# An attention softmax whose norms move ahead of the score diagonals, and value loads and transposes moved a period later

**The chip and the metric.** The kernel runs on one core of a Trainium2 chip. The time is the device time of one execution in microseconds (us), and where one number stands for several executions it is the median. A run is called slow when it is more than 1.5% above the fastest run of its kernel; medians and ranges below keep such runs, ratios leave them out. Engines are named as the profile names them: PE multiplies matrices, PEld loads its weights, DVE, ACT and POOL work on vectors, SP issues transfers. "PEq" and "SPq" are the instruction queues of PE and SP.

## The reference

Four batches of 6208 rows and 256 columns go through two stages. The attention is over channels, so its score matrix is 256 x 256 per batch, and its norms run over all rows.

```python
qn = q / (np.linalg.norm(q, axis=1, keepdims=True) + 1e-06)
kn = k / (np.linalg.norm(k, axis=1, keepdims=True) + 1e-06)
s = kn.transpose(0, 2, 1) @ qn / tau          # 256 x 256 per batch
a = softmax(s)                                # cut: written out in the reference
x = v @ a
x_prev = x moved down by one row              # cut
xk = mu_k * x + (1.0 - mu_k) * x_prev
xr = mu_r * x + (1.0 - mu_r) * x_prev
k = np.maximum(xk @ w_k, 0.0)                 # 256 -> 1024
out = sigmoid(xr @ w_r) * (k * k @ w_v)       # 1024 -> 256
```

## The kernel before

Nothing of `x` can be computed before the scores of its batch are complete, so the kernel has two parts. In the first some 34 us it reads all of q and k of batch 0, and sums the covariance and the squares as the rows land. Then comes a serial stretch: norms, square roots, scaling, transposes of the scaled scores, exp, weights, first product. After that 48 blocks of 512 rows follow one another, twelve per batch and a remainder. A stretch of work for one block is called a period here, some 10 us. The covariance of batches 1 to 3 is woven into the periods of the batch before.

The covariance of batch 0 in its last group of rows, and the norms, which came after everything else. The square of a query norm is a diagonal entry of q times q, and the diagonals are taken by a multiplication with the identity and a sum:

```python
def cov_first(g, diagonal=None):
    ...
    if last:
        for s in range(n):
            for ih in range(2):
                c = slice(at[ih], at[ih] + P)
                nc.tensor.matmul(cov[0][ih][:, c], row[:, s, c], row[:, s, c], ...)
        diagonal()
    ...
def norms_first():          # 22 matmuls of one column: sums of squares of k
    bank[0] = ps.tile([P, 4], F32, name="bank", tag="xT_ps", bufs=2)
    ...
def diagonals():
    for h in range(2):
        nc.vector.tensor_tensor(dg[:, h], cov[0][h][:, ...], ident_f, op=OP.mult)
    nc.vector.tensor_reduce(rn[:, 0:2], dg, axis=AX, op=OP.add)
```

The serial stretch, in program order:

```python
norms_first()
... # loads of v, w_k, w_r, w_v and of the next groups are issued
root(0)                                              # of the queries
root(1)                                              # of the keys
nc.scalar.activation(gate, ones[:, 0:1], AF.Exp)     # brings the exp table in
invert_first(0)
evac_first()                                         # scaling of the scores
go = v_transpose_pe(0, nc.vector.tensor_copy)        # v of block 0, on PE
...
turn()                                               # transposes of the scores
invert_first(1)
go()
...
exp()
v_transpose_pe(1, nc.scalar.copy)()
keep_warm(2)                                         # filler matmuls
weigh_first(0)
weigh_first(1)
...
```

In the main loop the v of a block is loaded by POOL (in bf16), transposed from one on-chip buffer into another by a transfer that SP issues, and used in the product `xT`. The results of a block go out by a store that SP issues too.

```python
if j == 0 and 4 <= i + 6 < NBLK - 1:
    v_load(i + 6)                  # v_bf: 6 buffers
...
if j == 5 and 4 <= i + 5 < NBLK - 1:
    v_transpose(i + 5)             # vT: 5 buffers, issued on SP
...
stores.append((dst, res))          # res: 6 slots; the first stores are held back (HOLD = 4)
while len(stores) > max(0, HOLD - max(0, i - 3)):
    nc.sync.dma_start(*stores.pop(0))          # issued on SP
```

Of the kernel before, what the change touches and what calls it, by code (L numbers as in the profile page):

```python
# [18 lines left out]
def kernel(  # L19
# [115 lines left out]
    def group_cast(g, between):  # L135
# [6 lines left out]
        else:  # L142
# [3 lines left out]
                              f[0][:rows, :n].rearrange("p s (x c) -> p s x c", c=P))  # L146
        if between:
            between.pop(0)()
# [29 lines left out]
    def cov_first(g, diagonal=None):  # L178
# [7 lines left out]
# [4 lines that stand above are left out]
                    nc.tensor.matmul(cov[0][ih][:, c], row[:, s, c], row[:, s, c], start=False, stop=s == n - 1,  # L190
                                     skip_group_check=True)
            diagonal()
        for s in range(n):
            for ih in range(2):
                c = slice(P, 3 * P) if last else slice(ih * P, ih * P + 3 * P)
                nc.tensor.matmul(cov[0][ih][:, c], row[:rows, s, at[ih]:at[ih] + P], row[:rows, s, c],  # L196
                                 start=g == 1 and s == 0, stop=last and s == n - 1, skip_group_check=True)

    def norms_first():

        bank[0] = ps.tile([P, 4], F32, name="bank", tag="xT_ps", bufs=2)
# [3 lines left out]
        for g in [0] + list(range(DIRECT, LAST + 1)):  # L205
            rows, n = rows_of(0, g)
            k2 = groups[0, g][1] if g else rowsum["left"]
            for s in range(n):
                for h in range(2):
                    nc.tensor.matmul(bank[0][:, h:h + 1], k2[:rows, s, h * P:(h + 1) * P], ones[:rows, 0:1],  # L210
                                     start=False, stop=g == LAST and s == n - 1, skip_group_check=True)
# [68 lines left out]
    def softmax_pieces(b):  # L280
# [18 lines left out]
        def diagonals():  # L299
            dg = pn.tile([P, 2, P], F32, name="dg", tag="dg", bufs=1)  # L300
            for h in range(2):
                nc.vector.tensor_tensor(dg[:, h], cov[0][h][:, 3 * P * h:3 * P * h + P], ident_f, op=OP.mult)
            nc.vector.tensor_reduce(rn[:, 0:2], dg, axis=AX, op=OP.add)
# [64 lines left out]
    L1 = L + 1  # L368
    HOLD = 4
# [6 lines left out]

    def v_load(i):
        b, t = blocks[i]
        v_bf = p2.tile([P, S, C], BF16, name="v_bf", tag="v_bf", bufs=6)
# [4 lines left out]
    def v_transpose(i):  # L384

        v_bf = st.pop((i, "v"))
        vT = p2.tile([P, S, 2, P], BF16, name="vT", tag="vT", bufs=5)
# [3 lines left out]
    def v_transpose_pe(i, evac):  # L391
# [7 lines left out]
        if i == 0:  # L399
            return lambda: evac(vT0[:, :, 1:].rearrange("c h (s p) -> c s h p", s=S), vT_ps)  # L400
        vT = p2.tile([P, S, 2, P], BF16, name="vT", tag="vT", bufs=5)
        st[i, "vT"] = vT
        if i == 3:
# [4 lines left out]
                            vT_ps.rearrange("c s h p -> c h p s"))  # L408

# [17 lines left out]

    H = M // 2
# [202 lines left out]
    for g in order(0):  # L631
        if (0, g) not in groups:
            group_load(0, g)
        if g == LAST:
            nc.sync.dma_start(mu_rows[0:2], moe_mu_k.rearrange("(h p) -> h p", p=P))
            nc.sync.dma_start(mu_rows[2:4], moe_mu_r.rearrange("(h p) -> h p", p=P))
        group_cast(g, pending)
        pending = k_sum(g) if 0 < g < DIRECT else []
        cov_first(g, diagonals)
        if g == NB - 1:  # L640

            nc.gpsimd.tensor_copy(gate, groups[0, g][0][:, 0, 0:1])
            v_load(0)
    norms_first()
# [52 lines left out]
    difference, product = x_first()  # L697
    root(0)
    root(1)
    nc.scalar.activation(gate, ones[:, 0:1], AF.Exp)  # L700
    invert_first(0)
    evac_first()
    go = v_transpose_pe(0, nc.vector.tensor_copy)
    mu_ps = ps.tile([P, 4], F32, name="mu_ps", tag="kT_ps", bufs=3)
    nc.tensor.transpose(mu_ps, mu_rows, ident_f[:4, :4])
    turn()
    invert_first(1)
    go()
    nc.vector.tensor_copy(mu_t, mu_ps)
# [3 lines left out]
    v_transpose_pe(1, nc.scalar.copy)()  # L713
    keep_warm(2)
# [15 lines left out]
    for i in range(-2, NBLK - 1):  # L730
        for j in range(8):
# [5 lines left out]
            if j == 0 and 4 <= i + 6 < NBLK - 1:  # L737
                v_load(i + 6)
# [41 lines left out]
            if j == 5 and 4 <= i + 5 < NBLK - 1:  # L780
                v_transpose(i + 5)
# [63 lines left out]
```

## Time and profile before

| | before |
|---|---|
| time, median of 3 runs | 505.6 us (505.32 to 506.75) |
| span of the profiled execution | 504.6 us, mean granted clock 0.997 |
| PE busy | 480.1 us, 95% |
| DVE and ACT busy | 85% each |
| PE wait from 60 to 490 us | none listed |
| last k of batch 0 landed | 34.47 us |

The lines themselves are shown and read in the prediction. The granted clock of PE is 1.00 when full and 0.50 when halved. A mean clock of 0.997 over 504 us means that one window of 3.41 us at half clock fell into this execution (half of 3.41 us is 1.7 us, and 1.7/504 is 0.0034). The trace places it from 38.29 to 41.70 us.

### The profile page before, as it was taken

The numbers are of one execution on the slowest core, as the hardware profiler recorded it, in microseconds if no ns is written. First come the engines' busy times: TensorE is split into PE (matmuls) and PEld (weight loads), VectorE is DVE, ScalarE is ACT, GpSimd is POOL, SyncE is SP. The second block draws the span as 40 slices with busy tenths as digits, with TensorE's granted clock in tenths as the row PEclk, the third lists the DMA queues.
The fourth block names the chain that finished last, engine by engine and source line by source line (L and its number), as shares of the span: only waits on it lengthen the run. The fifth ranks groups of instructions, "written<-read, shape, count | busy, mean of one in ns | idle before, by whom it ended". The sixth has DMA issues, their size and how long they took to land.

```text
span 504.6 us, 9229 instructions
## 1 busy us (share of the span) xinstructions
PE 480.1 (95%) x3370; PEld 332.0 (66%) x3429; DVE 430.1 (85%) x788; ACT 428.4 (85%) x869; POOL 96.7 (19%) x143
## 2 busy tenths in 40 slices
PE   1689999999999999999999999999999999999996
PEld 0355667667676676767676676667666666666675
DVE  2787899999989999899889899899988787878784
ACT  3778999899989988888999898988888878888784
POOL 0044332222233223112133322100031000000000
PEclk9998999999999999999999999999999999999999
DMA  8999999999999999997699999972296854452123
GB/s 323 419 314 198 196 164 163 159 201 205 232 216 161 215 172 170 163 185 115 141 188 156 177 189 185 162 155 63 64 205 113 153 98 110 81 100 70 54 73 105
DMA packets 131542, 83.46 MB, mean 165 GB/s; under 512 B 50532, under 2 KB 125608, under 8 KB 130472
## 3 DMA queue, kind: packets, MB, share of 16 engines
q0 software_dynamic: 55824, 33.01, 51.0%
q1 hardware_dynamic: 75352, 49.59, 42.8%
q8 instruction: 27, 0.44, 0.4%
q10 hardware_dynamic: 320, 0.26, 0.2%
q14 instruction: 19, 0.16, 0.1%
HBM read 78.71 MB, written 25.43 MB: 206 GB/s over the span
## 4 chain that ended last, share of the span: by engine, by line
PE 82%; DVE 6%; ACT 5%; DMA 5%; issue 2%; SPq 0%; POOL 0%; DVEq 0%; ACTq 0%
PE vr_ps L564 31%; PE kT_ps L532 28%; PE vr_ps L560 9%; PE xT_ps L424 7%; PE s_ps L277 5%; DMA f<-in_k_dram 4%; DVE kk L545 1%; ACT kr L537 1%; DVE xk L517 1%; ACT k L158 1%; DMA v_bf<-in_v_dram 1%; ACT sq L235 1%; DVE res L574 1%; ACT qk L153 1%; DVE delta L507 0%
## 5 line engine op out<-in xcount | busy, mean ns | idle before, releaser
L537 ACT ACTIVATE kr<-kT_ps 128x512 bf16<-128x512 f32 (+1 forms) x390 | 234.5, 603 | 33.6 <-PE kT_ps L532 29.7
L564 PE MATMUL vr_ps<-w_v_sb,kk 128*128 128x256 bf16 x1536 | 230.2, 273 | 0.4
L532 PE MATMUL kT_ps<-xk,w_k_sb 128*128 128x512 bf16 (+1 forms) x722 | 217.6, 377 | 0.3 <-DVE xk L517 0.2
L564 PEld LDWEIGHTS <-kk 128*128 128x128 bf16 x1536 | 150.3, 98 | 57.3
L545 DVE TENSOR_TENSOR kk<-kr 128x2048 bf16<-128x2048 bf16 (+1 forms) x148 | 125.8, 851 | 0.2 <-ACT kr L537 0.2
L574 DVE SCALAR_TENSOR_TENSOR res<-res,vr_ps 128x256 f32<-128x256 f32 x192 | 80.0, 417 | 50.2 <-ACT res L573 50.2
L532 PEld LDWEIGHTS <-w_k_sb 128*128 128x128 bf16 x780 | 75.5, 98 | 27.5 <-issue 0.6
L573 ACT ACTIVATE res<-vr_ps 128x256 f32<-128x256 f32 x192 | 76.4, 398 | 1.3 <-PE vr_ps L564 1.3
L560 PE MATMUL vr_ps<-w_r_sb,xr 128*128 128x256 bf16 x384 | 73.3, 273 | 2.5
L426 ACT CAST xT<-xT_ps 128x512 bf16<-128x512 f32 x94 | 55.9, 594 | 20.0 <-PE xT_ps L424 19.6
L517 DVE SCALAR_TENSOR_TENSOR xk<-delta,mu_t,xT 128x512 bf16<-128x512 bf16 x94 | 70.0, 746 | 0.0
L517 DVE SCALAR_TENSOR_TENSOR xr<-delta,mu_t,xT 128x512 bf16<-128x512 bf16 x94 | 70.0, 746 | 0.0
L560 PEld LDWEIGHTS <-xr 128*128 128x128 bf16 x384 | 37.6, 98 | 44.6 <-issue 0.2
L133 POOL DMA_DIRECT2D qk<-in_q_dram x39 | 26.0, 667 | 161.8 <-ACT kr L537 142.9
L424 PE MATMUL xT_ps<-vT,a_sb 128*128 128x512 bf16 x188 | 55.9, 379 | 0.0
L277 PE MATMUL s_ps<-qk 128*128 128x256 bf16 (+1 forms) x294 | 55.8, 273 | 0.0
L238 ACT ACTIVATE sq<-qk 128x1024 bf16<-128x1024 bf16 x48 | 51.0, 1062 | 0.0
L380 POOL DMA_DIRECT2D v_bf<-in_v_dram x48 | 36.5, 764 | 50.5 <-DMA vT<-v_bf 39.7
L196 PE MATMUL s_ps<-qk 128*128 128x384 bf16 (+2 forms) x98 | 19.7, 349 | 16.3 <-ACT qk L153 15.4
L507 DVE TENSOR_TENSOR delta<-xT 128x1024 bf16<-128x1024 bf16 x47 | 32.3, 686 | 1.1 <-ACT xT L426 1.1
L277 PEld LDWEIGHTS <-qk 128*128 128x128 bf16 (+1 forms) x294 | 28.5, 98 | 5.6 <-issue 0.8
L133 POOL DMA_DIRECT2D qk<-in_k_dram x39 | 25.8, 662 | 8.2 <-DMA v_bf<-in_v_dram 3.5
(110 smaller groups left out, 252.7 us busy)
## 6 DMA issues: line engine op xcount, KB each, us to landing
out_dram<-res SPq DMA_DIRECT2D x47, 512.0 KB, 4.8
v_bf<-in_v_dram POOLq DMA_DIRECT2D x48, 256.0 KB, 8.4
qk<-in_q_dram POOLq DMA_DIRECT2D x36, 256.0 KB, 7.2
qk<-in_k_dram POOLq DMA_DIRECT2D x36, 256.0 KB, 8.8
f<-in_q_dram SPq DMA_DIRECT2D x4, 1024.0 KB, 13.5
f<-in_k_dram SPq DMA_DIRECT2D x4, 1024.0 KB, 11.0
f<-in_q_dram SPq DMA_DIRECT2D x3, 512.0 KB, 7.7
f<-in_k_dram SPq DMA_DIRECT2D x3, 512.0 KB, 6.2
```

What stands on the lines that cost most here:

```text
L133: nc.gpsimd.dma_start(rows_at(qk, b, g, i)[:rows, :n], qk_src(t, b, g))
L277: nc.tensor.matmul(s_ps[:, ih, :], rows_at(qk, b, g, 0)[:rows, s, ih * P:(ih + 1) * P], rows_at(qk, b, g, 1)[:rows, s, :], start=t0 and ih ...
L424: nc.tensor.matmul(xT_ps, a_sb[:, b, ih, dh * P:(dh + 1) * P], vT[:, :, ih, :], start=ih == 0, stop=ih == 1)
L426: nc.scalar.copy(xT[:, dh, 1:], xT_ps)
L517: nc.vector.scalar_tensor_tensor(o[:, dh], st[i, "d"][:, dh], mu[:, dh:dh + 1], st[i, "x"][:, dh, :M], op0=OP.mult, op1=OP.add)
L532: nc.tensor.matmul(kT_ps[:, :m], w_k_sb[:, dh, fh * P:(fh + 1) * P], xk[:, dh, :m], start=dh == 0, stop=dh == 1)
L537: nc.scalar.activation(kr, kT_ps[:, :m], AF.Relu, scale=0.5 ** 0.5)
L545: nc.vector.tensor_tensor(st[i, "kk"][:, fh // 4 * 4 + lo:fh + 1, :m], kr, kr, op=OP.mult)
L560: nc.tensor.matmul(vr_ps[:, D:], xr[:, dh, s * P:(s + 1) * P], w_r_sb[:, dh, :], start=dh == 0, stop=dh == 1)
L564: nc.tensor.matmul(vr_ps[:, :D], kk[:, fh, s * P:(s + 1) * P], w_v_sb[:, fh, :], start=fh == 0, stop=fh == 7)
L573: nc.scalar.activation(res[:, s], vr_ps[:, D:], AF.Tanh, scale=0.5)
L574: nc.vector.scalar_tensor_tensor(res[:, s], res[:, s], 1.0, vr_ps[:, :D], op0=OP.add, op1=OP.mult)
```

## The change

The intent has two parts. In the start, everything that the exp table waits for is moved forward, and the v of block 0 comes in two halves. In the main loop v is loaded and transposed one period later, so that two transposed buffers do and fewer transfers queue up. Its core, with cuts:

```diff
 def cov_first(g, diagonal=None):
             diagonal()
+            norms_last()            # 4 of the 22 norm matmuls, behind the diagonals
...
-            nc.vector.tensor_tensor(dg[:, h], cov[0][h][:, ...], ident_f, op=OP.mult)
-        nc.vector.tensor_reduce(rn[:, 0:2], dg, axis=AX, op=OP.add)
+            nc.vector.scalar_tensor_tensor(dg[:, h], cov[0][h][:, ...], 1.0, ident_f,
+                                           op0=OP.mult, op1=OP.mult, accum_out=rn[:, h:h + 1])
...
+        if g == LAST:
+            norms_first()           # the other 18, ahead of the last group
         group_cast(g, pending)
         cov_first(g, diagonals)
         if g == NB - 1:
-            nc.gpsimd.tensor_copy(gate, groups[0, g][0][:, 0, 0:1])   # POOL marker
             v_load(0)               # after: a DVE memset marks it; loaded in two halves
-norms_first()
...
-    root(0)
     root(1)
+    root(0)
     nc.scalar.activation(gate, ones[:, 0:1], AF.Exp)
+    nc.tensor.transpose(bank[0][:, 4:8], mu_rows, ident_f[:4, :4])
+    keep_warm(2)
+    turn_half, take_half = v_first()
     invert_first(0)
     evac_first()
-    go = v_transpose_pe(0, nc.vector.tensor_copy)
...
+    turn_half(0)
     turn()
+    turn_half(1)
+    go = v_transpose_pe(1, nc.scalar.copy)
+    keep_warm(3)
     invert_first(1)
-    go()
+    take_half(0, nc.vector.tensor_copy)
...
     exp()
-    v_transpose_pe(1, nc.scalar.copy)()
-    keep_warm(2)
+    take_half(1, nc.scalar.copy)
+    go()
...
-            if j == 0 and 4 <= i + 6 < NBLK - 1:
-                v_load(i + 6)                       # v_bf: 6 buffers
+            if j == 0 and 4 <= i + 5 < NBLK - 1:
+                v_load(i + 5)                       # 5 buffers
...
-            if j == 5 and 4 <= i + 5 < NBLK - 1:
-                v_transpose(i + 5)                  # vT: 5 buffers
+            if j == 5 and 4 <= i + 4 < NBLK - 1:
+                v_transpose(i + 4)                  # 2 buffers
```

The line numbers shift. L190 (diagonal matmuls) becomes L192, L203 and L210 (norms) L206 and L217, L306 (roots) L317, L316 (scaling) L327, L337 (transposes of the scores) L348, L345 (exp) L356, L448 (first product) L482, L388 (transposes by transfer) L411, L573 and L581 (tanh into the result, store) L607 and L615.

More of the change, by code (lines that the diff above doesn't have):

```diff
@@ L146, in group_cast @@
                               f[0][:rows, :n].rearrange("p s (x c) -> p s x c", c=P))
+        if g == NB - 1:
+            v_mark()
         if between:
@@ L199, in norms_first @@
     def norms_first():
-        bank[0] = ps.tile([P, 4], F32, name="bank", tag="xT_ps", bufs=2)
+        bank[0] = ps.tile([P, 8], F32, name="bank", tag="xT_ps", bufs=2)
         for h in range(2):
@@ L204, in norms_first, with norms_of, norms_last @@
                              start=h == 0, stop=False, skip_group_check=True)
-        for g in [0] + list(range(DIRECT, LAST + 1)):
-            rows, n = rows_of(0, g)
-            k2 = groups[0, g][1] if g else rowsum["left"]
-            for s in range(n):
-                for h in range(2):
-                    nc.tensor.matmul(bank[0][:, h:h + 1], k2[:rows, s, h * P:(h + 1) * P], ones[:rows, 0:1],
-                                     start=False, stop=g == LAST and s == n - 1, skip_group_check=True)
+        for g in [0] + list(range(DIRECT, LAST)):
+            norms_of(g)
+    def norms_of(g):
+        rows, n = rows_of(0, g)
+        k2 = groups[0, g][1] if g else rowsum["left"]
+        for s in range(n):
+            for h in range(2):
+                nc.tensor.matmul(bank[0][:, h:h + 1], k2[:rows, s, h * P:(h + 1) * P], ones[:rows, 0:1],
+                                 start=False, stop=g == LAST and s == n - 1, skip_group_check=True)
+    def norms_last():
+        norms_of(LAST)
     def half_tile(name, shape, dtype, tag):
@@ L301, in diagonals @@
             for h in range(2):
-                nc.vector.tensor_tensor(dg[:, h], cov[0][h][:, 3 * P * h:3 * P * h + P], ident_f, op=OP.mult)
-            nc.vector.tensor_reduce(rn[:, 0:2], dg, axis=AX, op=OP.add)
+                nc.vector.scalar_tensor_tensor(dg[:, h], cov[0][h][:, 3 * P * h:3 * P * h + P], 1.0, ident_f,
+                                               op0=OP.mult, op1=OP.mult, accum_out=rn[:, h:h + 1])
         def root(h):
@@ L368 @@
     L1 = L + 1
+    H = M // 2
     HOLD = 4
@@ L375, in size, with v_mark @@
         return M if i < NBLK - 1 else B * L
+    def v_mark():
+        st["mark"] = p2.tile([P, S, C], BF16, name="v_bf", tag="v_bf", bufs=5)
+        nc.vector.memset(st["mark"][0:1, 0, 0:1], 0.0)
     def v_load(i):
         b, t = blocks[i]
-        v_bf = p2.tile([P, S, C], BF16, name="v_bf", tag="v_bf", bufs=6)
+        v_bf = st.pop("mark") if i == 0 else p2.tile([P, S, C], BF16, name="v_bf", tag="v_bf", bufs=5)
+        if i == 0:
+            for a in range(2):
+                nc.gpsimd.dma_start(v_bf[:, 2 * a:2 * a + 2], v[b, a * H:(a + 1) * H, :].rearrange(
+                    "(s p) c -> p s c", p=P))
+            st[i, "v"] = v_bf
+            return
         nc.gpsimd.dma_start(v_bf, v[b, t * M:(t + 1) * M, :].rearrange(
@@ L386, in v_transpose @@
         v_bf = st.pop((i, "v"))
-        vT = p2.tile([P, S, 2, P], BF16, name="vT", tag="vT", bufs=5)
+        vT = p2.tile([P, S, 2, P], BF16, name="vT", tag="vT", bufs=2)
         nc.sync.dma_start_transpose(vT.rearrange("c s h p -> c (s h) p"), v_bf.rearrange("p s c -> p (s c)"))
@@ L397, in v_transpose_pe @@
                 nc.tensor.transpose(vT_ps[:, s, h], v_bf[:, s, h * P:(h + 1) * P], ident)
-        if i == 0:
-            return lambda: evac(vT0[:, :, 1:].rearrange("c h (s p) -> c s h p", s=S), vT_ps)
-        vT = p2.tile([P, S, 2, P], BF16, name="vT", tag="vT", bufs=5)
+        vT = p2.tile([P, S, 2, P], BF16, name="vT", tag="vT", bufs=2)
         st[i, "vT"] = vT
@@ L408, in v_transpose_pe, with v_first, turn_half, take_half @@
                             vT_ps.rearrange("c s h p -> c h p s"))
+    def v_first():
+        v_bf = st.pop((0, "v"))
+        vT_ps = ps.tile([P, S, 2, P], BF16, name="vT_ps", tag="kT_ps", bufs=3)
+        def turn_half(a):
+            for s in (2 * a, 2 * a + 1):
+                for h in range(2):
+                    nc.tensor.transpose(vT_ps[:, s, h], v_bf[:, s, h * P:(h + 1) * P], ident)
+        def take_half(a, copy):
+            copy(vT0[:, :, a * H + 1:(a + 1) * H + 1].rearrange("c h (s p) -> c s h p", s=2),
+                 vT_ps[:, 2 * a:2 * a + 2])
+        return turn_half, take_half
     def x_half(i, dh):
@@ L426, in x_half @@
         nc.scalar.copy(xT[:, dh, 1:], xT_ps)
-    H = M // 2
     def x_first():
@@ L697 @@
     difference, product = x_first()
+    root(1)
     root(0)
-    root(1)
     nc.scalar.activation(gate, ones[:, 0:1], AF.Exp)
+    nc.tensor.transpose(bank[0][:, 4:8], mu_rows, ident_f[:4, :4])
+    keep_warm(2)
+    turn_half, take_half = v_first()
     invert_first(0)
     evac_first()
-    go = v_transpose_pe(0, nc.vector.tensor_copy)
-    mu_ps = ps.tile([P, 4], F32, name="mu_ps", tag="kT_ps", bufs=3)
-    nc.tensor.transpose(mu_ps, mu_rows, ident_f[:4, :4])
+    turn_half(0)
     turn()
+    turn_half(1)
+    go = v_transpose_pe(1, nc.scalar.copy)
+    keep_warm(3)
     invert_first(1)
-    go()
-    nc.vector.tensor_copy(mu_t, mu_ps)
+    take_half(0, nc.vector.tensor_copy)
+    nc.vector.tensor_copy(mu_t, bank[0][:, 4:8])
     nc.vector.tensor_scalar_add(less, mu_t, -1.0)
```

## The prediction

> **What bounds the kernel now.** I first read the busy totals, then the list of waits, then the windows, and then the timeline of the start. The page's totals and its costliest matmul groups:
>
> ```profile
> PE 480.1 (95%) x3370; PEld 332.0 (66%) x3429; DVE 430.1 (85%) x788; ACT 428.4 (85%) x869; POOL 96.7 (19%) x143
> ...
> L564 PE MATMUL vr_ps<-w_v_sb,kk 128*128 128x256 bf16 x1536 | 230.2, 273 | 0.4
> L532 PE MATMUL kT_ps<-xk,w_k_sb 128*128 128x512 bf16 (+1 forms) x722 | 217.6, 377 | 0.3 <-DVE xk L517 0.2
> ```
>
> PE is busy 95% of the span, and its two large groups waited 0.7 us in all (the numbers after the second bar). The list of PE's waits confirms it: its longest entry is 15.4 us for the ACT cast of L153, and its window from 60 to 490 us lists no PE wait at all. So after the start the kernel runs at the pace of the matmul stream. Two whole periods (one period is one block of 512 rows) from the windows view; the columns are window, length, busy time of PE, PEld, DVE, ACT and POOL, then granted clock, DMA share and GB/s:
>
> ```profile
> 110.44:120.55 10.11, 10.01 (x76) 7.18 (x76) 9.78 (x19) 9.28 (x20) 3.79 (x6) 1.00 1.34 203
> 343.06:352.74 9.68, 9.58 (x72) 6.79 (x72) 8.76 (x17) 8.56 (x19) 0.00 (x0) 1.00 0.38 82
> ```
>
> The first has 20 matmuls of 512 columns and 52 of 256 (six covariance units in it), the second 8 fewer of 256. Both are full; the DMA engines are saturated in the first (share above 1) and idle most of the time in the second.
>
> What is left to win is the start, the first 50 us, where one chain goes through several engines. The end of it, from the timeline (start, duration, engine, line):
>
> ```profile
> 34.88 0.39 PE L190 MATMUL s_ps<-qk 128*128 128x128 bf16 x4
> 35.24 0.49 DVE L302 TENSOR_TENSOR dg<-s_ps,ident_f 128x128 f32<-128x128 f32 x2 [0.32 <-PE s_ps L190]
> 35.77 0.42 DVE L303 TENSOR_REDUCE rn<-dg 128x2 f32<-128x256 f32 x1
> 36.11 0.50 PE L203 MATMUL bank<-ones_f,k_acc 128*128 128x1 f32 x4
> 36.93 0.88 DVE L316 TENSOR_SCALAR s_sb<-s_ps,rn 128x256 f32<-128x256 f32 x2
> 37.27 0.17 ACT L306 ACTIVATE rn<-bank 128x2 f32<-128x2 f32 x1 [0.84 <-PE bank L210]
> 37.41 0.62 PE L397 MATMUL vT_ps<-ident,v_bf 128*128 128x128 bf16 x8 [0.18 <-DMA v_bf<-in_v_dram]
> 37.46 1.28 ACT L700 ACT_TABLE_LOAD   x1
> 38.11 0.99 PE L337 MATMUL st_ps<-ident_f,s_sb 128*128 128x128 f32 x4
> 39.14 0.47 ACT L345 ACTIVATE e_sb<-st_ps,rn 128x256 f32<-128x256 f32 x1 [0.18 <-PE st_ps L337]
> 40.60 0.64 PE L448 MATMUL x_ps<-vT,a_sb 128*128 128x256 bf16 x2 [0.22 <-DVE sm L357]
> ```
>
> The key norms and roots come after everything else, the v of block 0 holds PE until 37.4, and the transposes of the scaled covariance (L337) release exp. From 38 to 42 us PE runs at half clock, which the windows view shows:
>
> ```profile
> 34.70:38.10 3.40, 2.90 (x42) 2.33 (x39) 2.60 (x11) 1.52 (x4) 3.40 (x6) 1.00 1.16 171
> 38.10:41.60 3.50, 3.28 (x19) 2.59 (x20) 2.50 (x10) 2.77 (x7) 1.15 (x2) 0.53 1.08 190
> ```
>
> **What the Trainium skill says.** "TensorE: Matmul & The Clock Gate", Back-to-back issue gap, gives N/2.4 + 2.5 ns for a warm matmul. An estimate for the first period above is then 20 x 0.2158 + 52 x 0.1092 = 9.99 us; the trace has 10.0 to 10.1, so it agrees, and the stream holds no slack to win. The same page, Part 1: The HAM clock gate, says the clock is halved after a window of about 3.4 us with little PE activity, and that the window runs freely. The trace agrees: 0.53 for 3.5 us, and matmuls of 128 columns 0.107 us apart in it against 0.056 before. "ScalarE: Activation LUTs", What ACT_TABLE_LOAD costs, gives 1283 ns for the load; the trace has 1.28. "DMA: Bandwidth & Descriptors", Queues, rings and completion order, says each DMA engine takes turns between queue rows and consumes one ring in order. The trace agrees in so far as transposes issued behind stores landed late: 17.5 us after issue for the one at 110.9 us, against 3.1 at the least in a quiet stretch.
>
> **The change, part by part.**
>
> Norms ahead. The instruction order shows 18 tiny matmuls (4 f32 passes, then 14 of k squares) moved in front of L190. Before, the 22 tiny matmuls took from 36.11 to 37.1, so the 18 take about 0.9 us. PE is continuously busy up to L190 (its L196 matmuls run from 32.88 into 34.88), so nothing hides them: L190 goes from 34.88 to about 35.75, a loss of 0.9 on the path to the diagonals.
>
> Diagonals. The multiply with accumulated sum removes the reduce: 35.24 to 36.19 is 0.95 us now, about 0.55 after. A gain of 0.4. The query root would then come at about 36.7 instead of 36.2.
>
> Roots. With the key root first (at about 36.4) and the query root last (until 36.9), the table load starts at about 36.95, not 37.46, a gain of 0.5 on ACT: ready for exp at 38.45, not 38.96.
>
> v of block 0. Its marker is one DVE memset after an early cast, in place of a POOL copy that waited for the key cast and ended at 32.28; the first half may be issued at about 31.9, not 32.4, and lands by my estimate at 35.5. So L337 no longer stands behind eight transposes. It waits for the scaled covariance: invert and scaling start 0.45 later than now (36.93 to about 37.4), its two halves are ready at 37.9 and 38.3, and the transposes end at about 38.7 with a full clock, 38.95 with half. They end at 39.1 now. Exp thus gains 0.15 to 0.4 us.
>
> After exp. Two bf16 copies stand on ACT (half of v, 0.55 us, and the v of block 1, 1.01 us) before the first xT cast, which can start near 41.4 at best against 42.00 now. Three filler matmuls stand before the first product. With a full clock they and the 12 transposes cost 0.65 + 0.67 us and end at about 40.0, before the weights are ready. With half clock they cost 1.28 + 1.28, and the first product starts at 41.4, not 40.6. So the sum of the start is a gain of about 0.6 us if the clock stays up, and a loss of about 0.6 if not. The two fillers added at about 37 raise activity by 0.43 us in a window of 3.4; I cannot tell from one trace whether this is enough, and call it 60 to 40 for it. Expected: 0.6 x 0.6 - 0.4 x 0.6 = 0.1 us gained, and with the relief of the first DMA burst (one v load and one transpose fewer before 60 us) I call it 0.3.
>
> Later v. No instruction more or less. The two vT buffers tie a transpose for block n to the end of the product of block n-2. Its lead is two periods less the 3.2 us that this product is spread over: 16.8 us where the period is 10, 16 later. In the trace landing takes 4 to 11 us after 140 us, so 5 us or more remain. Between 60 and 130 us landing took 16.4 to 19.1 us from issue. That is not service time alone: three transposes stood in one ring, and they landed 6 to 10 us apart. Issued one per period they should land in 7 to 10 us up to 100 us, and in 13 to 16 behind two stores of 512 KB each around 110 to 140 us. Slack is thus 1 to 8 us: tight, but positive, so I count nothing for it.
>
> **Sum**: 505.6 - 0.3 = 505.3; I say 505.2.
>
> **Rivals.**
> 1. Late vT. If a transpose lands in 18 us as now, PE waits about 1 us in each of the periods from 60 to 140 us, and up to 10 us in all: 507 to 515. For it: the landing times. Against it: with fewer transposes queued the ring is shorter, and total DMA work by any moment falls.
> 2. Half clock with fillers in the way: 506.2, as worked out above. For it: 0.53 in the window. Against it: the fillers were put there to prevent it.
> 3. The start gains more: no half clock at all, and the later v frees the burst for weights and q, k: 504.0. For it: DMA share above 1 from 42 to 130 us. Against it: from 60 us on no PE wait is listed, so earlier data has nothing to shorten there.
>
> **Range and chances.** 2% is 10 us. The start can give little more than 1.5 us, as PE is full from 50 us on, so faster by 2% is all but excluded. Only rival 1 in its worst form reaches 2% slower. The range 503.6 to 507.2 holds rivals 2 and 3 and a mild form of rival 1.
>
> **What would show it.** L190's counterpart starts near 35.75; the table load near 36.95; exp near 38.8; the first product near 40.1 (right) or 41.4 (rival 2); the granted clock from 38 to 41.6 near 1 or near 0.5. A list of PE waits from 60 us on with entries for the vT transposes would prove rival 1, and periods between 60 and 140 us above 10.1 us would size it. If block 3's product starts later than 60.3 us with the clock up, my reading of the start is wrong.

## The result

| | before | after |
|---|---|---|
| time in the same rounds | 506.18 us (505.32 to 507.29, 4 runs) | 505.73 us (505.47 to 506.17, 4 runs) |
| ratio, 95% interval | | 0.9991 (0.9967 to 1.0015): same |
| span and clock, profiled | 504.6 us, 0.997 | 503.7 us, 0.998 |

A ratio is the mean time of one kernel's fast runs over that of the other's of the same rounds, so it is not quite the ratio of the medians. The output is correct. The medians differ by less than the runs of one kernel do. What differs more is the scatter, and the experiments return to it.

The page of the changed kernel has the busy totals, and the groups, almost unchanged. The columns of the groups are: line, engine, operation, count, then busy time, mean ns of one, and idle time before them.

```profile
PE 479.2 (95%) x3372; PEld 331.1 (66%) x3432; DVE 428.9 (85%) x790; ACT 428.7 (85%) x870; POOL 97.0 (19%) x143
...
L598 PE MATMUL vr_ps<-w_v_sb,kk 128*128 128x256 bf16 x1536 | 230.3, 273 | 0.1
L566 PE MATMUL kT_ps<-xk,w_k_sb 128*128 128x512 bf16 (+1 forms) x721 | 217.3, 377 | 0.4 <-DVE xk L551 0.2
```

The two groups of matmuls stand at 230.3 and 217.3 us, as before. PE lists no wait from 60 to 490 us in this kernel either. The windows of the start do differ: the granted clock (the seventh number after the window) is now full in the second one, where it was 0.53.

```profile
34.70:38.10 3.40, 2.98 (x39) 2.28 (x39) 1.75 (x9) 1.99 (x5) 3.40 (x7) 1.00 1.00 137
38.10:41.60 3.50, 3.01 (x29) 2.14 (x29) 2.39 (x11) 2.78 (x9) 1.27 (x2) 1.00 1.03 164
```

These lines are picked out of the serial stretch in the timeline of the changed kernel (start, duration, engine, line; the bracket is idle time before the instruction and what ended it):

```profile
34.69 0.50 PE L206 MATMUL bank<-ones_f,k_acc 128*128 128x1 f32 x4
35.26 0.45 PE L217 MATMUL bank<-ones,k 128*128 128x1 bf16 x12
35.57 0.38 PE L192 MATMUL s_ps<-qk 128*128 128x128 bf16 x4
35.94 0.29 DVE L313 SCALAR_TENSOR_TENSOR dg<-s_ps,ident_f 128x128 f32<-128x128 f32 x1 [1.27 <-PE s_ps L192]
36.37 0.08 DVE L313 DVE_READ_ACCUMULATOR dg<-s_ps,ident_f 128x1 f32 x1
36.71 1.28 ACT L734 ACT_TABLE_LOAD   x1
37.74 0.83 PE L348 MATMUL st_ps<-ident_f,s_sb 128*128 128x128 f32 x4
38.41 0.39 PE L439 MATMUL vT_ps<-ident,v_bf 128*128 128x128 bf16 x4
38.61 0.47 ACT L356 ACTIVATE e_sb<-st_ps,rn 128x256 f32<-128x256 f32 x1 [0.40 <-PE st_ps L348]
38.83 0.42 DVE L442 COPY vT<-vT_ps 128x512 bf16<-128x512 bf16 x1 [0.48 <-PE vT_ps L439]
39.97 0.35 DVE L369 TENSOR_SCALAR a_sb<-e_sb,sm 128x256 bf16<-128x256 f32 x1
40.38 0.39 PE L482 MATMUL x_ps<-vT,a_sb 128*128 128x256 bf16 x2 [0.49 <-DVE a_sb L369]
```

The norms (L206, L217) run from 34.69 until the diagonal matmuls (L192) can start at 35.57, so they cost 0.88 us with nothing beside them. The table load then starts at 36.71, not 37.46, and exp at 38.61, not 39.14. Yet the first product starts at 40.38, only 0.22 us sooner than before, and the last k alone landed 0.27 us sooner in this run (34.20 against 34.47). Counted from that landing, the first product is 0.05 us **later** than before (6.18 against 6.13 us).

The reason is in the line of L442. DVE's copy of the first half of v starts when the PE transposes of the *second* half end (38.41 + 0.39 = 38.80), although it needs only the first: both halves lie in one tile. That copy and the work queued behind it put the weights (L369) at 39.97, and PE waited 0.49 us for them. The runs norms_mid and better, below, test this: with both halves in one tile the copy starts at 38.32, when the second half's transposes have ended, and with a tile for each it starts at 37.90, before those transposes begin (38.09).

The gain that the profile does show comes after that. The product of block 1 starts 9.60 us after the last k, against 10.07 before, because PE is no longer at half clock from 38.29 to 41.70. The product of block 3 then keeps that distance: 25.32 against 25.79. So the 0.9 us between the two spans are 0.47 from the start, 0.27 from the landing of the data, and 0.16 from the rest.

In the main loop, the instruction queue of SP looks different. First before, then after, picked from the timeline (L388 and L411 are transposes, L581 and L615 are stores; the second number is how long the issue took):

```profile
93.60 4.84 SPq L581 DMA_DIRECT2D out_dram<-res  x2
98.55 9.90 SPq L388 DMA_TRANSPOSE vT<-v_bf  x1
108.54 2.23 SPq L581 DMA_DIRECT2D out_dram<-res  x2
```

```profile
92.94 1.23 SPq L411 DMA_TRANSPOSE vT<-v_bf  x1
94.27 1.49 SPq L615 DMA_DIRECT2D out_dram<-res  x2
102.93 1.33 SPq L411 DMA_TRANSPOSE vT<-v_bf  x1
104.31 1.66 SPq L615 DMA_DIRECT2D out_dram<-res  x2
```

Before, a transpose took 9.90 us merely to be issued, and two stores took 4.84 us. After, it is 1.2 to 1.3 us and 1.5 to 1.7 us. The transposes issued between 90 and 125 us landed 17.5 to 18.3 us after issue before, and 4.5 to 7.5 us after. PE sees none of this in these two profiles; the experiments show where it matters.

### The profile page after: what moved, and what is told of

The parts are those of the page before. It is cut to its first block, busy times and chain, and to the rows that moved or that the text cites. A ratio compares the mean times of both kernels' runs of the same rounds, so it can differ in the third digit from the quotient of the medians.

```text
span 503.7 us, 9236 instructions
## 1 busy us (share of the span) xinstructions
PE 479.2 (95%) x3372; PEld 331.1 (66%) x3432; DVE 428.9 (85%) x790; ACT 428.7 (85%) x870; POOL 97.0 (19%) x143
## 4 chain that ended last, share of the span: by engine, by line
PE 90%; DMA 4%; ACT 2%; DVE 2%; issue 1%; SPq 0%; ACTq 0%; DVEq 0%
PE vr_ps L598 33%; PE kT_ps L566 30%; PE vr_ps L594 10%; PE xT_ps L460 8%; PE s_ps L288 6%; DMA f<-in_k_dram 4%; ACT k L160 1%; ACT qk L155 1%; PE s_ps L199 1%; PE st_ps L348 0%; PE y_ps L638 0%; DVE xk L551 0%; DVE k L167 0%; DVE kk L579 0%; ACT kr L508 0%
## 5 line engine op out<-in xcount | busy, mean ns | idle before, releaser
L598 PE MATMUL vr_ps<-w_v_sb,kk 128*128 128x256 bf16 x1536 | 230.3, 273 | 0.1
L566 PE MATMUL kT_ps<-xk,w_k_sb 128*128 128x512 bf16 (+1 forms) x721 | 217.3, 377 | 0.4 <-DVE xk L551 0.2
L607 ACT ACTIVATE res<-vr_ps 128x256 f32<-128x256 f32 x192 | 76.6, 399 | 1.3 <-PE vr_ps L598 1.3
```

What stands on the lines that cost most here:

```text
L566: nc.tensor.matmul(kT_ps[:, :m], w_k_sb[:, dh, fh * P:(fh + 1) * P], xk[:, dh, :m], start=dh == 0, stop=dh == 1)
L598: nc.tensor.matmul(vr_ps[:, :D], kk[:, fh, s * P:(s + 1) * P], w_v_sb[:, fh, :], start=fh == 0, stop=fh == 7)
L607: nc.scalar.activation(res[:, s], vr_ps[:, D:], AF.Tanh, scale=0.5)
```

## The experiments

Two questions are to be told apart. Theory: the new start saves nothing of its own and only avoids a half-clock window, and the later v is what keeps the scatter away. Rivals: the new order of the start is itself worth about half a microsecond; or the later v is neutral, as the prediction counted it. The expectations for the first runs still favoured these rivals, and v_only and start_only speak against them.

All times of the start below are counted from the landing of the last k in the same profile, because that landing moves by up to 0.5 us from run to run (34.16 to 34.68 us) and has nothing to do with the change. Every kernel gave a correct result.

| kernel | exp | first product | block 1 | block 3 | block 9 | half clock in the start |
|---|---|---|---|---|---|---|
| before | 4.67 | 6.13 | 10.07 | 25.79 | 86.08 | 3.41 us |
| after | 4.41 | 6.18 | 9.60 | 25.32 | 85.62 | none |
| after_again | 4.44 | 6.21 | 9.63 | 25.36 | 85.65 | none |
| start_only | 4.49 | 6.25 | 9.71 | 25.44 | 88.25 | none |
| v_only | 4.20 | 5.45 | 8.87 | 24.59 | 84.89 | none |
| before_warm | 4.53 | 5.73 | 9.16 | 24.88 | 85.70 | none |
| tr_only | 4.55 | 6.31 | 9.74 | 25.46 | 85.75 | none |
| hold2 | 4.43 | 6.20 | 9.62 | 25.35 | 85.64 | none |
| more_res | 4.36 | 6.13 | 9.55 | 25.27 | 85.56 | none |
| norms_mid | 3.86 | 5.65 | 9.46 | 25.18 | 85.47 | none |
| better | 3.79 | 5.55 | 9.39 | 25.11 | 85.40 | none |
| better_one | 4.79 | 6.17 | 9.62 | 25.35 | 85.64 | none |
| after_nofill | 4.31 | 8.10 | 12.84 | 28.56 | 88.85 | 6.83 us |

The columns are the start of the instruction in question in us: exp, the first product of block 0, and the first product of blocks 1, 3 and 9.

### The changed kernel again

No edit; this only sets the scatter, in five rounds.

> The changed kernel unaltered, to size the difference and to see how often each kernel drops to half clock at the start. Theory (the start alone gains, part of it by keeping the clock up): ratio to the kernel before 0.998 to 1.000, first product of block 0 about 40.4 us after the start of the span, block 3's first xT product near 59.5 us (60.26 before), no half clock between 30 and 60 us in any profile. Rival (the 0.9 us between the two spans is chance, of the load phase and of where a free-running clock window happens to fall): ratio 1.000 within 0.1%, and the granted clocks of the two kernels' runs spread alike.

Measured: 505.75 us (505.62 to 506.03, 6 runs). The kernel before, in the same rounds, had a median of 505.79 and a range of 505.04 to 513.03 in 11 runs; the ratio is 0.9975 (0.9926 to 1.0024). The medians are equal, and the lowest run of before is below the lowest of the changed kernel by 0.58 us. Four of the eleven runs of before were 507 us or more. So the change does not make a good run better, and the next runs ask what it does to a bad one.

### The new start with the old v, and the old start with the new v

start_only has the changed kernel's start, and the loads, transposes and buffers of the old loop:

```diff
-name="v_bf", tag="v_bf", bufs=5        # after
+name="v_bf", tag="v_bf", bufs=6
-name="vT", tag="vT", bufs=2
+name="vT", tag="vT", bufs=5
-v_load(i + 5) ... v_transpose(i + 4)
+v_load(i + 6) ... v_transpose(i + 5)
```

v_only is the reverse: the same four edits the other way round, made to the kernel before.

> The changed start with the old v schedule (v loaded and transposed one period earlier, 6 and 5 buffers). Theory (all of the gain is the start): within 0.1% of the changed kernel, block 3's product near 59.5 us, and the transposes of 60 to 130 us land 16 to 19 us after issue again. Rival (the later v gives the gain by relieving the first burst): block 3's product back near 60.2 us, time back to that of the kernel before.

> The old start with the new v schedule (one period later, 5 and 2 buffers). Theory: same time as the kernel before within 0.1%, block 3's product near 60.3 us, no PE wait from 60 us on, transposes of 80 to 130 us land 4 to 8 us after issue as in the changed kernel. Rival 1 of the prediction (late vT): PE waits for transposes appear. Rival (v gives the gain): 0.15% faster than the kernel before.

Measured: start_only 508.99 us (505.76 to 510.67, 6 runs; ratio 1.0026, 0.9973 to 1.0079), v_only 505.16 us (504.95 to 505.38, 6 runs; ratio 0.9963, 0.9919 to 1.0008). In the same rounds the changed kernel ran 505.62 to 506.03, so v_only is faster than it in every run, if only by about 0.6 us, or 0.1%. Two of the six runs of start_only (505.76 and 505.97) are as fast as the changed kernel, and four are 508.5 or more; its profile is of one of the four.

The start first. v_only keeps the old start, and its profile happened to have the full clock without any added filler:

```profile
34.70:38.10 3.40, 3.07 (x45) 2.56 (x43) 2.78 (x11) 1.62 (x4) 3.40 (x6) 1.00 1.18 169
38.10:41.60 3.50, 2.66 (x27) 1.90 (x27) 2.71 (x11) 3.26 (x9) 1.16 (x2) 1.00 1.06 183
```

At full clock the old start is quicker than the new one. Its exp (38.88 in its own time, from a landing at 34.68) and its first product are these lines of its timeline:

```profile
38.88 0.46 ACT L345 ACTIVATE e_sb<-st_ps,rn 128x256 f32<-128x256 f32 x1
...
40.13 0.39 PE L448 MATMUL x_ps<-vT,a_sb 128*128 128x256 bf16 x2 [0.38 <-DVE sm L357]
```

The first product stands 5.45 us after the last k, against 6.18 in the changed kernel, and block 3 stands at 24.59 against 25.32: 0.73 us better in both. So the new start wins only against the old start at half clock, and the rival that its order is worth half a microsecond falls.

Now the loop. With the old v, start_only lost 2.5 us between block 3 and block 9 (88.25 - 25.44 = 62.81 us, against 85.62 - 25.32 = 60.30 in the changed kernel). Its SP queue, its ACT timeline and its list of PE waits from 60 to 140 us:

```profile
97.69 4.19 SPq L615 DMA_DIRECT2D out_dram<-res  x2
101.99 11.32 SPq L411 DMA_TRANSPOSE vT<-v_bf  x1
```

```profile
117.30 0.38 ACT L607 ACTIVATE res<-vr_ps 128x256 f32<-128x256 f32 x1 [3.37 <-DMA out_dram<-res]
...
PE vr_ps L594 <- DVE res L608: 2.2, 2, 1.8
```

The store of block 1 was issued late behind transposes, and landed at 117.22. The results of two blocks share a buffer, and there are three buffers (six slots), so block 6 takes the buffer of blocks 0 and 1. ACT sat idle for 3.37 us until the store of block 1 was out, and PE then waited 2.2 us in two places. In the profile of before the same store landed at 112.55 and the buffer was written again at 114.19: **1.64 us of slack**, and no wait. In other words, the old schedule ran close to a stall, and a run in which the transfers are a little later pays for it.

### Half clock alone: before with two fillers

```diff
+    keep_warm(2)
     go = v_transpose_pe(0, nc.vector.tensor_copy)
```

> The kernel before with two filler matmuls of 512 columns put ahead of the PE transposes of block 0's v, nothing else. Theory (the half clock of 38.3 to 41.7 us is worth about half of the start's gain): no half clock in the profile, first product of block 0 at about 40.2 us instead of 40.6, block 3's product near 59.9 us. Rival (the clock costs nothing since other waits end last there): the clock is full and block 3's product stays at 60.2 to 60.3. If the half clock is still there, two fillers were not what kept it up in the changed kernel.

Measured: 505.61 us (505.15 to 506.07, 6 runs), ratio 0.9972 (0.9927 to 1.0017). The clock was full in its profile, here in the windows of the start:

```profile
34.70:38.10 3.40, 3.00 (x42) 2.38 (x41) 2.57 (x10) 1.43 (x4) 3.40 (x6) 1.00 1.12 161
38.10:41.60 3.50, 3.15 (x29) 2.31 (x30) 2.79 (x10) 3.30 (x9) 1.08 (x2) 1.00 1.07 188
```

Block 3 came 24.88 us after the last k, 0.91 us sooner than in before (25.79) and 0.44 sooner than in the changed kernel (25.32), from one added pair of fillers. That puts a half-clock window in the start at 0.9 us, by one pair of profiles. The store of block 1 landed at 114.57 here, and its buffer was wanted 1.38 us before that: ACT idled 1.38 us, and PE waited 0.4 us. So part of the gain is given back under the old v schedule: block 9 stands at 85.70, only 0.38 better than before. The quicker start is the smaller part of it. The buffer was wanted 0.92 us sooner than in before (113.27 against 114.19), but the store landed 2.02 us later, and why it did is not shown.

### Which part of the later v: held stores, transposes, or result slots

Three variants of start_only. hold2 lets the first stores go earlier, tr_only moves only the transposes, more_res gives the results another pair of slots (the same buffers hold loads of q in the first part, so these get one more too):

```diff
-    HOLD = 4                              # hold2
+    HOLD = 2
```

```diff
-    vT ... bufs=5;  v_transpose(i + 5)    # tr_only; loads stay at i + 6
+    vT ... bufs=2;  v_transpose(i + 4)
```

```diff
-    res pairs (tag f0) ... bufs=3         # more_res: 8 slots instead of 6
+    res pairs (tag f0) ... bufs=4
```

> The changed start with the old v schedule, as in start_only, and two held-back stores instead of four, so that the first stores go out about 20 us earlier. Theory (the stalls of start_only and of the slow runs before are tanh writing block 6's result into a buffer whose store, stuck behind transposes in one queue, has not landed): first store issued near 74 us instead of 97.7, no idle time of ACT before block 6's first tanh (3.37 us in start_only), block 9's xT product near 120.1 us (122.66), all runs within 505.5 to 506.3 (start_only 505.8 to 510.7). Rival (the stall is the DMA load as such, v and q, k arriving late): stalls and times as in start_only.

> The changed start, v loaded as in the kernel before (one period earlier than in the changed kernel, 6 buffers), transposes as in the changed kernel (a period later, two vT buffers). Theory (the queue that transposes and stores share is what counts): store of block 1 takes under 1 us to issue, transposes of 80 to 130 us land 4 to 8 us after issue, no stall, runs within 505.5 to 506.3 as the changed kernel. Rival (fewer v loads in the burst do it): stalls as in start_only, 506 to 510.

> start_only (changed start, old v schedule) with one more buffer pair for results: 8 result slots instead of 6, nothing moved in the queues. It takes the disputed wait away by another buffer. Theory (the stall is the reuse of a result slot whose store has not landed): transposes land as late as in start_only (16 to 21 us after issue in 60 to 130 us) and the store of block 1 still takes about 18 us, but no wait of the matmul stream from 60 us on, block 9's xT product 60.3 us after block 3's (62.8 in start_only), runs within 505.5 to 506.5. Rival (something else in the burst stalls it): times of 508 to 510 in more than half of the runs as in start_only.

Measured: hold2 506.03 us (505.77, 505.98, 506.08 and one of 512.21), tr_only 505.73 us (505.66 to 505.98, 4 runs), more_res 506.02 us (505.73, 505.76, 505.87, 506.18, 506.56 and one of 513.72). In all three the stall of 2.5 us is gone from the profile: block 9 stands at 85.64, 85.75 and 85.56. tr_only has the short queue of the changed kernel again:

```profile
93.05 1.23 SPq L411 DMA_TRANSPOSE vT<-v_bf  x1
94.38 1.17 SPq L615 DMA_DIRECT2D out_dram<-res  x2
```

So later transposes alone are enough, with the loads where they were. And more_res shows the chain to be the right one from its other end: its store of block 1 still landed late, at 117.93, but its buffer wasn't wanted yet, and ACT did not wait.

What stays open: under the old v schedule single runs are 5 to 8 us longer than the rest (513.72 in more_res, 512.21 in hold2, and five of 44 runs of before are above 510). Neither another slot nor earlier stores removed them, so it isn't the wait that the profile of start_only shows, or not it alone. No profile fell into such a run. What the runs show is only that none occurred where the transposes are a period later: 38 runs of seven such kernels with at least two vT buffers and their fillers or the old start (after, after_again, v_only, tr_only, norms_mid, better, better_one) lie between 504.58 and 506.17. That is a count and not a proof: before_warm, with the old v schedule, had no such run in six either (505.15 to 506.07).

### The order of the norms, and a better start

norms_mid puts all norms behind the diagonal matmuls and in front of the rest of the last group, and the query root first:

```diff
             diagonal()
+            norms_first()
             norms_last()
...
-        if g == LAST:
-            norms_first()
...
-    root(1)
     root(0)
+    root(1)
```

better is norms_mid with the halves of block 0's v in tiles of their own (on both sides of the copy), and with the copy of mu moved behind the weights. better_one is better with block 0's v loaded whole again:

```diff
-        vT_ps = ps.tile([P, S, 2, P], ...)                                  # better
+        vT_ps = [ps.tile([P, 2, 2, P], ...) for _ in range(2)]
-    vT0 = const.tile([P, 2, M + 1], ...)
+    vT0 = [const.tile([P, 2, M // 2 + 1], ...) for a in range(2)]
...
-            for a in range(2):                                              # better_one
-                nc.gpsimd.dma_start(v_bf[:, 2 * a:2 * a + 2], v[b, a * H:(a + 1) * H, :]...)
+            nc.gpsimd.dma_start(v_bf, v[b, :M, :]...)
```

> The changed kernel with its 18 early norm matmuls put behind the diagonal matmuls instead of ahead of them, and the query root first. Theory (ahead of the diagonals they cost the 0.88 us that they take, on the path): diagonal matmuls about 0.85 us earlier than in the changed kernel measured from the landing of the last k, exp 0.5 to 0.8 us earlier, block 3's product 0.3 to 0.7 us earlier. Rival (they hide in the wait of the path for something else, the table or v): exp within 0.2 us of where it is.

> norms_mid, and after exp: block 0's v in two tiles of its own per half, so that the copy of the first half does not wait for the PE transposes of the second, nor the first product for the copy of the second; mu copied after the weights. Theory (in the changed kernel the first product waited for DVE, which had begun the copy of v late, at 38.8 us): first product 1.2 to 1.4 us after exp starts (1.77 in the changed kernel), block 3's product 24.0 to 24.5 us after the last k has landed (25.3 to 25.4 in the changed kernel, 24.6 with the old start at full clock), time 504.6 to 505.1. Rival (the ACT copies after exp set the path anyway): product to block 3 no shorter than in norms_mid.

> The kernel of run better with v of block 0 loaded whole instead of in two halves. Theory (in norms_mid and better the first up-projection starts the moment w_k has landed, 0.85 to 0.9 us after its input is ready, because the second half costs one more DMA issue of 0.9 us ahead of w_k): w_k issued near 33.6 us and landed near 42.0, the first up-projection within 0.3 us of its input, block 1's product 8.6 to 8.9 us after the last k has landed (9.39 in better), block 3's 24.3 to 24.6, time 504.4 to 505.0. Rival (w_k lands when the burst lets it, not when it is issued): w_k still at 42.6 or later, nothing won.

Measured: norms_mid 505.31 us (505.0 to 505.57), better 505.43 (504.96 to 505.92), better_one 505.15 (504.58 to 505.65), six runs each.

In norms_mid exp stands 0.55 us earlier than in the changed kernel, at 3.86 against 4.41, and the first product 0.53 us. So the norms ahead of the diagonals, with the order of the roots that goes with them, cost about half a microsecond on the path, of the 0.88 that they take. Yet block 1 gains only 0.14 us. The timeline of norms_mid shows what took over:

```profile
42.62 0.61 PE L507 MATMUL kT_ps<-xk,w_k_sb 128*128 128x256 bf16 x4 [0.79 <-DMA w_k_sb<-in_moe_w_k_dram]
```

The first up-projection waited for the weights w_k, which landed at 42.57, while its other operand was ready at 41.73. better, quicker still up to the first product (5.55), meets the same wait (w_k landed at 42.76). The second half of v costs one more issue in the queue ahead of w_k. better_one takes it out: w_k was issued at 33.57 (34.26 in norms_mid) and landed at 41.81. But now the whole v lands only at 38.11, the transposes of the scores stand behind those of v on PE, and exp comes at 4.79. In these three runs, then, the start is bound by what the first burst of transfers brings in which order: what norms_mid and better won on PE and DVE was lost again in the wait for w_k, and what better_one won at w_k was lost in the wait for v. All three missed what was expected of block 3 (0.3 to 0.7 us gained, then 24.0 to 24.5 and 24.3 to 24.6; measured 25.18, 25.11 and 25.35). The tiles of their own that better gives the two halves were worth 0.10 us at the first product (5.55 against 5.65). In medians all three lie 0.3 to 0.6 us below the changed kernel, partly in other rounds, which is at the edge of what the runs resolve (their ratios to the kernel before are 0.9988, 0.9992 and 0.9979, with 0.9964 to 0.9993 for the last). With v_only, better_one has the lowest median; the two differ by 0.01 us, and neither is better than the kernel before by more than 0.4%.

### One vT buffer less, to size the risk

```diff
-        vT = p2.tile([P, S, 2, P], BF16, name="vT", tag="vT", bufs=2)
+        vT = p2.tile([P, S, 2, P], BF16, name="vT", tag="vT", bufs=1)
```

> The changed kernel with one vT buffer instead of two: a transpose can then be issued only after the product of the block just before it. To size the slack that the prediction called tight. The lead falls from 16.8 to 6.8 us where a period is 10; the transposes of the changed kernel landed 4.5 to 13 us after issue. Theory: PE waits for transposes nearly everywhere landing takes over 6 us, several us per block between 60 and 300 us; 530 to 620 us in all. Rival (landing shrinks further with one transpose in flight, to about 4 us): under 510 us.

Measured: 537.62 us (533.37 to 542.78, 4 runs), ratio 1.0621 (1.0558 to 1.0683). The line from its waits:

```profile
PE xT_ps L460 <- DMA vT<-v_bf: 20.9, 10, 3.9
```

PE waited for the transposes 20.9 us in ten places (3.9 at most). The profiled run is 27.8 us longer than that of the changed kernel (531.5 against 503.7): besides those waits it has three windows of 3.41 us at half clock, from 74.20, 169.77 and 296.07 us, worth at most half of their length, 5.1 us in all, which leaves some 2 us unplaced. The run of the median has 4 us more, of which no profile was kept. With two buffers, a transpose has 3.45 to 12.4 us of slack in the changed kernel, taken from its landing to the product that uses it, up to 140 us. So two is enough and one is not.

### The fillers

```diff
-    keep_warm(2)          # after, ahead of the halves of block 0's v
```

> The changed kernel without the two filler matmuls that it runs ahead of block 0's v. Theory of the prediction (they keep the clock up): half clock for 3.4 us somewhere between 35 and 42 us, first product about 1 us later than in the changed kernel. Rival (the half clock of the kernel before was the chance of where a free-running window fell; the run v_only had the old start, no fillers and a full clock): full clock from 14 us on, first product 6.0 to 6.25 us after the last k has landed, as with the fillers (6.18 and 6.21), time within 0.1% of the changed kernel.

Measured: 506.6 us (505.6 to 509.25, 5 runs; ratio 0.999, 0.9919 to 1.0061). Three of the five runs have a clock of 0.997 or less, against none of the ten runs of the changed kernel with fillers (0.998 to 1.0). The profile shows two windows at half clock, and PE waiting for v besides:

```profile
38.10:41.60 3.50, 2.20 (x20) 1.91 (x22) 2.59 (x12) 1.99 (x7) 2.09 (x3) 0.58 0.99 169
41.60:45.00 3.40, 3.18 (x14) 1.93 (x14) 0.28 (x2) 1.66 (x3) 1.06 (x3) 0.50 1.18 206
```

Block 3 comes at 28.56 here, 3.2 us later than with them. Part of that is v, for which PE waited 1.9 us in this run (1.3 in one place and 0.6 in another), though the edit doesn't touch its loads; how much each part weighs was not separated. By the clocks of the runs, the fillers do hold the clock up in the new start. But the old order with the same pair of fillers (before_warm) has a full clock in its profile too, and is 0.44 us ahead at block 3.

## Why the prediction was right or wrong

The number was right: 505.2 predicted, 505.73 measured, inside the range of 503.6 to 507.2. Part of that is luck: the runs don't resolve a gain of 0.4 us (the ratio's interval is 0.9967 to 1.0015), and the sum rests on a comparison that failed. By its own steps:

- **PE bound, nothing to win after 50 us.** Right for the profiles of before and after: no PE wait is listed from 60 to 490 us in either. Its working has two slips. The second of its two windows has 4 matmuls of 256 columns fewer than the first (48 against 52), not 8, and its estimate leaves out four of 65 columns, which each window has: with them the same formula gives 10.11 us for the first, the window's length. The page gives this formula for a matmul on its own and says that it over-counts in a stream; here the stream follows it, with 216 ns from start to start at 512 columns (median of 480 pairs from 60 to 490 us in before; 215.8 by the formula).
- **Norms ahead, 0.9 us on the path.** Right: 0.88 us. The diagonals start at 35.57, for 35.75.
- **Diagonals, 0.55 us.** Right: from 35.94 to 36.45 is 0.51 us.
- **Roots and table.** Right: 36.71 for 36.95.
- **Exp, 0.15 to 0.4 us sooner.** Right: 0.26 us counted from the last k (4.41 against 4.67), and exp starts at 38.61 for 38.8. But this too is against an old start at half clock: at full clock, in v_only, the old order has exp at 4.20, ahead of the new.
- **First product near 40.1.** Wrong: 40.38, which is near in absolute time only. Counted from the last k, 40.1 would have been 5.63 and it came at 6.18, so half a microsecond was expected and nothing won. The prediction counted fillers, transposes and copies on ACT, and left out DVE's copy of half 0. It waits for half 1, as both are in one tile, and PE then waits 0.49 us for the weights.
- **The start gains 0.6 us if the clock stays up.** The size was near, 0.47 us, and the mechanism was wrong. This is the step that failed. The prediction set the new start at full clock against an old start at half clock. It did make the gain hang on the clock of the new start, but never asked what the old order does at full clock, and so counted as the change's gain what the clock gave. before_warm and v_only show the old order at full clock: it is 0.44 and 0.73 us *better* than the new. The gain is the clock's, 0.9 us for one window, and part of the runs of before have a mean clock of 0.998 to 1.000, with no such window. That fits medians that hardly differ.
- **Later v, nothing counted.** Right for the waits that it looked at, and short in what it looked at. The prediction asked whether a transpose would come too late for its product. It did not ask what the early transposes do to the stores behind them in the same queue. start_only shows it: 3.37 us of idle ACT at a result slot, where before had 1.64 us of slack.
- **Landing of transposes in 7 to 16 us.** Too long: 4.5 to 8 us between 70 and 130 us (the one issued at 62.75 took 12.7). The old 18 us were queueing to a greater part than the prediction took. After 140 us it was too short at one place: the transpose issued at 153.11 took 12.2 us where 4 to 11 were expected, and kept 3.6 us of slack.
- **Rival 1, late vT.** Fell with two buffers; vt1 shows what it would have been.
- **Rival 2, half clock with fillers in the way.** Fell: clock 1.00 from 13.8 us to the end of the stretch. after_nofill shows that it was near.
- **Rival 3, the start gains more.** Fell as well: block 3 gained 0.47 us, not 1.6.

Where the expected gain went, then: the start's gain is really the avoidance of a half-clock window that only some runs have, and it costs the 0.4 to 0.7 us by which the new order is behind the old at full clock in the profiles. The later v saves little in a good run. What the runs show besides is a narrower scatter. Over all five sessions 19 of the 44 runs of before are above 506.3 us (7 of 15 in the two sessions with the changed kernel), and none of the 10 runs of the changed kernel. This is a count. Which half of the change narrows it is not shown, as before_warm, with the old order and the old v and only a pair of fillers more, stayed below 506.3 too. And neither of the two causes alone explains all of it: part of those runs carry half-clock windows, one or two by their mean clock (0.995 to 0.997), and those above 510 us carry the part that stays open.

## What to carry to other kernels

Before crediting a new order with a gain, run the old order at the same clock: a pair of cheap fillers in the old kernel tells the two apart. A transfer issued early isn't free, because it holds up what is issued behind it on the same queue: look at how long the issue itself takes, and at the slack of the slowest buffer behind it. When two halves are to be handled separately, give each a tile of its own, or the first can wait for the second, as here (though it was worth only 0.1 us in better).

## What the Trainium skill lacked or had wrong

- "DMA: Bandwidth & Descriptors", DMA Transpose (X-bar), gives the constraints on a transposing transfer, and the page has bandwidths and, for earlier generations, a cycle count per tile for transposes elsewhere, but nothing on how long the issue takes in a busy queue. Here 256 KB took 1.23 to 1.33 us to issue in the later schedule (after) and 4.5 to 11.3 us in the early one (before and start_only, all between 89 and 116 us), with landings 4.5 to 7.5 and 16.4 to 19.6 us after issue, and what came behind it on SP was issued only after it.
- "TensorE: Matmul & The Clock Gate", Part 1: The HAM clock gate, calls the window that halves the clock idle, and doesn't say how much work such a window may hold. Its length of about 3.4 us agrees (3.41 us here). Busy time doesn't settle it. By the profile PE was busy for 2.91 of the 3.41 us ahead of the half clock in before (34.88 to 38.29), and for only 1.71 us in an earlier window of the same run (17.81 to 21.22) and 1.46 us in one of hold2 (21.74 to 25.15), after which the clock stayed full. Counted by the columns of the matmuls that started in them, the order is the expected one: 2,842 ahead of the half clock, 22 of the 41 matmuls being one column wide, and 3,840 and 3,072 in the other two. That is a count of three windows, and not a rule.
- "ScalarE: Activation LUTs", What ACT_TABLE_LOAD costs, adds about 1380 ns of drain to 1283 ns for each switch. The load is 1.28 us here, but the drain doesn't show: in after ACT's root ended at 36.69, the load ran from 36.71 to 37.99, and the next ACT instruction started at 38.00.
